# A gated mix of an S4D convolution and a GLU: a new table for the order of every engine

## The chip, the cores and the metric

The kernel runs on one core of a Trainium2 chip, in fp32 from end to end. A core has five engines with an instruction queue each, run in order: TensorE (PE in the profile, with its weight loads as PEld), VectorE (DVE), ScalarE (ACT), GpSimd (POOL) and SyncE (SP), which here only issues transfers to the DMA engines. An engine waits on semaphores for what other engines or transfers have to finish first. What counts is the device time of one execution in microseconds.

## The reference

One input u of 2048 positions by 448 channels goes through two branches and a gate. The first branch is a state-space convolution (S4D) of 256 states per channel, the second a GLU with 1792 hidden units.

```python
def _A_ref(u, log_A_real, A_imag, C_real, C_imag, log_dt, D_skip):
    dt = jnp.exp(log_dt)
    A = -jnp.exp(log_A_real) + 1j * A_imag
    C = (C_real + 1j * C_imag) * dt[:, None]
    P = jnp.exp((A * dt[:, None])[:, :, None] * pos[None, None, :])
    K = 2.0 * jnp.einsum("dn,dnl->dl", C, P).real
    L2 = 2 * L
    ...
    y = jnp.fft.irfft(Uf * Kf[None, :, :], L2)[:, :, :L]
    ...
    return y + u * D_skip[None, None, :]
...
    g = jnp.einsum("bsd,df->bsf", x, w_gate)
    u = jnp.einsum("bsd,df->bsf", x, w_up)
    h = _sigmoid(g) * u
    return jnp.einsum("bsf,fd->bsd", h, w_down)
...
g = _sigmoid((x * gate_w).sum(-1, keepdims=True))
return g * a + (1 - g) * b
```

## The kernel before

Three strands of work share the engines, and the program interleaves them.

**The GLU** has the largest part of TensorE. The positions are split in two halves H of 1024, the hidden units in 14 groups f of 128. fp32 accuracy is had from pairs of rounded numbers: each weight and input is split into a high and a low part (L1341 to L1348 for x, L1379 and L1381 for the weights), and three products of high and low parts replace one. `glu_mm` writes one 128x512 tile `gu` in PSUM with eleven matmuls (L1414 to L1419; two gu buffers); ACT takes a tanh of it into `sg` (L1398), DVE multiplies (L1400, L1403), and the result is split into `hh` and `hl` (L1405, L1406) or, in the groups named in `WHOLE`, kept whole in fp32. `glu_down` multiplies by w_down into the one PSUM tile `dn` (three matmuls a group, L1435 to L1437; one fp32 matmul, L1433, for a whole group), and DVE or ACT adds it, scaled by the gate, to `ob` (L1445, L1452).

**The convolution kernel** K is generated in 28 chunks `c` (`kgen`), 16 channels at a time, in two half chunks of 128 states (`half_chunk`). The phase of every state is a product of position and frequency on TensorE, one 128x512 tile `tp` in PSUM (T1, L1223). ACT rounds it to whole turns (L1227) into `cs` and writes the negated turns `nn` (L1229); TensorE adds these to the same tile (T2, L1232), so that a fraction of a turn is left; ACT reads that for cosine (L1234) and sine (L1235, and L1245 for both halves of the cosine). GpSimd makes the decay as powers (L1203 to L1216), DVE spreads them (`es`, L1252) and multiplies them with cosine and sine (L1266, L1269). Then 128 small matmuls (L1281, in the mode of 128x32 tiles) contract over the states into `kp`, and ACT copies that to `ke` (L1302). There are two `tp` buffers, one `nn`, one `es`, three `cs` and one `kp`.

**The transforms** replace the FFT by two stages of matrices, 64 by 32, over position: stage 1 (L812, matmuls on 64 rows of the array), a transpose (for the input through DMA, for the kernel on DVE, L826), a spectrum stage (L845, 64x64 tiles), the product with the spectrum of the input (L879, DVE), the inverse stage (L889, 64x64) and the way back (L926, 64 columns). The matrices of the outer stages come from DRAM in tables `ft` (for the input half `fu`) and `ftx`, 256 KB a load; the `fu` strand and `ftx` have one buffer each, so a load waits until the last matmul of the table before is done, and the first of the next waits for the load.

**What sets the order.** All operations are first recorded with their reads, writes and buffers. `Plan.order` gives each operation the rank that the table `PLACE` has for it: the key is the engine, the tile that is written and a priority, and the numbers are the ranks on that engine of the operations with this key, in order of recording. Each engine's queue is sorted by this rank (`queue`), and the queues are emitted as they stand. A rank is not a time: an engine that comes to an instruction too early waits on its semaphore. Buffers of a tag rotate in the order of recording. The table therefore sets, for each engine, what stands between a producer and its consumer, and nothing else in the program does.

## Time and profile before

| | us |
|---|---|
| median of three runs | 690.57 |
| lowest, highest | 689.83, 692.58 |
| span of the profiled execution | 688.4 |
| PE busy in it | 673.8 (98%) |
| DVE, ACT, POOL busy | 602.0 (87%), 510.0 (74%), 274.9 (40%) |

The profiled execution is one of its own, 2.2 us shorter than the median. Its granted TensorE clock is full throughout. A busy share says how much of the time an engine had an instruction in work; with overlapping instructions of one engine the busy times of the groups sum to more than that. What an engine waits for, and how long, stands in the views of waits and in brackets in the timeline.

### The profile page before, as it was taken

The page shows a single profiled execution, that of the slowest core. Times are in us where ns is not written, and L with a number is a line of the kernel's source. Part 1 is how long each engine was busy: PE and PEld are TensorE (multiplying, and loading weights), DVE is VectorE, ACT ScalarE, POOL GpSimd, SP SyncE. Part 2 cuts the span into 40 slices and gives each one's busy share as a digit, 9 for nine tenths or more (in the row PEclk, how much of TensorE's full clock was granted, in tenths as well). Part 3 has the DMA queues.
Part 4 walks back from the last instruction along what each step waited for, and adds up shares of the span by engine and source line. Part 5 has one row for each costly group of instructions (what it writes and reads, how often), then busy time and mean ns, then how long its engine had stood idle before and what let it go on. Part 6 is the DMA issues. An engine that isn't in the chain of part 4 may idle for free.

```text
span 688.4 us, 16283 instructions
## 1 busy us (share of the span) xinstructions
PE 673.8 (98%) x6588; PEld 483.1 (70%) x6588; DVE 602.0 (87%) x699; ACT 510.0 (74%) x928; POOL 274.9 (40%) x280
## 2 busy tenths in 40 slices
PE   9999999999999999999899999999999999999996
PEld 8776667877886687775556676788888766556873
DVE  5999999999999999989999789999973489577976
ACT  5677699899999999999999999999941352233110
POOL 0315268865447656675663845667000000000000
PEclk9999999999999999999999999999999999999999
DMA  9769342656896787737966974457948973979866
GB/s 252 180 177 246 87 108 70 153 138 237 186 182 157 177 215 178 225 112 177 193 171 144 233 199 90 140 168 184 180 100 202 271 235 124 312 246 241 166 179 165
DMA packets 97474, 123.84 MB, mean 180 GB/s; under 512 B 31096, under 2 KB 80568, under 8 KB 96376
## 3 DMA queue, kind: packets, MB, share of 16 engines
q1 hardware_dynamic: 97400, 122.81, 69.8%
q8 instruction: 52, 0.85, 0.5%
q14 instruction: 22, 0.18, 0.1%
HBM read 79.20 MB, written 43.58 MB: 178 GB/s over the span
## 4 chain that ended last, share of the span: by engine, by line
PE 73%; ACT 10%; DVE 8%; DMA 5%; issue 2%; SPq 1%; ACTq 0%; DVEq 0%
PE gu_gps L1414 9%; PE gu_gps L1415 8%; PE gu_gps L1416 8%; PE kp_egp L1281 6%; PE dn_gps L1433 5%; PE dn_gps L1435 4%; PE tp_egp L1232 4%; PE dn_gps L1436 4%; PE dn_gps L1437 4%; PE tp_egp L1223 4%; PE fps_fups L812 3%; PE gu_gps L1418 3%; PE gu_gps L1419 3%; PE fps_fups L845 2%; PE fps_fups L889 2%
## 5 line engine op out<-in xcount | busy, mean ns | idle before, releaser
L1414 PE MATMUL gu_gps<-xs_glu,wh_glu 128*128 128x512 f32 x336 | 144.5, 430 | 1.4 <-DVE hl_glu L1400 0.9
L1416 PE MATMUL gu_gps<-xs_glu,wl_glu 128*128 128x512 f32 x336 | 131.8, 392 | 0.0
L1415 PE MATMUL gu_gps<-xs_glu,wh_glu 128*128 128x512 f32 x336 | 131.7, 392 | 0.0
L1269 DVE TENSOR_TENSOR cs_eg<-cs_eg,es_eg 128x2048 f32<-128x2048 f32 x56 | 129.2, 2307 | 1.4
L1252 DVE TENSOR_TENSOR es_eg<-tb_eg 128x1024 f32<-128x1024 f32 x112 | 110.5, 1003 | 3.0 <-POOL tb_eg L1216 0.9
L1213 POOL TENSOR_TENSOR tb_eg<-tb_eg 128x96 f32<-128x96 f32 (+2 forms) x84 | 107.5, 1284 | 5.9
L1216 POOL TENSOR_TENSOR tb_eg<-tb_eg,bs_eg 128x32 f32<-128x32 f32 x84 | 83.9, 1001 | 5.8
L1414 PEld LDWEIGHTS gu_gps<-xs_glu,wh_glu 128*128 128x128 f32 x336 | 63.2, 188 | 30.2 <-issue 13.0
L1398 ACT ACTIVATE sg_glu<-gu_gps 128x512 f32<-128x512 f32 x56 | 33.7, 603 | 58.3 <-PE gu_gps L1419 58.3
L1266 DVE TENSOR_TENSOR cs_eg<-cs_eg,es_eg 128x1024 f32<-128x1024 f32 x56 | 70.5, 1260 | 7.2 <-ACT cs_eg L1245 6.0
L1229 ACT ACTIVATE nn_eg<-cs_eg 128x512 fp32r<-128x512 f32 x112 | 71.7, 640 | 4.5 <-PE tp_egp L1232 2.9
L1415 PEld LDWEIGHTS gu_gps<-xs_glu,wh_glu 128*128 128x128 f32 x336 | 63.3, 188 | 15.4 <-issue 4.8
L1416 PEld LDWEIGHTS gu_gps<-xs_glu,wl_glu 128*128 128x128 f32 x336 | 63.1, 188 | 14.5
L1452 DVE SCALAR_TENSOR_TENSOR ob_glu<-dn_gps,og,ob_glu 128x448 f32<-128x448 f32 x72 | 48.7, 676 | 25.1 <-PE dn_gps L1437 24.1
L1234 ACT ACTIVATE cs_eg<-tp_egp 128x512 f32<-128x512 f32 x112 | 66.5, 605 | 4.1 <-PE tp_egp L1232 3.6
L1227 ACT ACTIVATE cs_eg<-tp_egp 128x512 f32<-128x512 f32 x112 | 67.9, 607 | 1.6 <-PE kp_egp L1281 0.6
L1235 ACT ACTIVATE cs_eg<-tp_egp 128x512 f32<-128x512 f32 x112 | 67.3, 606 | 1.6 <-PE tp_egp L1232 1.4
L1245 ACT ACTIVATE cs_eg<-cs_eg,half_pi 128x1024 f32<-128x1024 f32 x56 | 65.2, 1165 | 0.4
L1281 PEld LDWEIGHTS kp_egp<-cs_eg 128*32 128x32 f32 x3584 | 51.5, 110 | 11.7 <-issue 6.3
L1281 PE MATMUL kp_egp<-cs_eg 128*32 128x64 f32 x3584 | 56.3, 220 | 0.5 <-issue 0.4
L1203 POOL MEMSET tb_eg<- 128x96 f32 x28 | 7.8, 285 | 116.4 <-DVE es_eg L1252 105.5
L1232 PE MATMUL tp_egp<-nn_eg,idn 128*128 128x512 f32 x112 | 49.7, 444 | 3.9 <-ACT nn_eg L1229 3.4
(161 smaller groups left out, 1326.2 us busy)
## 6 DMA issues: line engine op xcount, KB each, us to landing
shf<-fx_fu SPq DMA_DIRECT2D x16, 896.0 KB
fx_fu<-shf SPq DMA_DIRECT2D x16, 896.0 KB
us<-fx_fu SPq DMA_DIRECT2D x16, 896.0 KB
xr_glu<-in_w_dram SPq DMA_DIRECT2D x46, 256.0 KB
uax_fk<-us SPq DMA_DIRECT2D x16, 448.0 KB
ua_fk<-us SPq DMA_DIRECT2D x16, 448.0 KB
xr_glu<-in_w_dram SPq DMA_DIRECT2D x17, 224.0 KB
gt_pre<-in_u_dram SPq DMA_DIRECT2D x8, 448.0 KB
```

Source lines behind the costliest of these rows:

```text
L1213: pool(96 * m, lambda n=n, m=m: G.tensor_mul(g3(n + 1, m), g3(1, m), g3(n, 1).to_broadcast([128, 32, 3, m])))
L1216: pool(32, lambda e=e: G.tensor_mul(t(e + 1), t(e), b(3)))
L1227: op("Act", c_act(512, True), lambda: S.activation(cs[:, 1, ds, 32:96], block(tp), AF.Copy, bias=MAGIC), [tp], [(cs, ("s", i))], prio)
L1229: op("Act", c_act(512), lambda: S.activation(block(nn), cs[:, 1, ds, 32:96], AF.Copy, scale=-1.0, bias=MAGIC), [(cs, ("s", i))], [nn], prio)
L1232: op("PE", c_mm(532), lambda: T.matmul(tp.real, idn.real, nn.real, start=False, stop=True, skip_group_check=True), [nn, idn], [tp], prio)
L1252: V.tensor_mul(o.rearrange("p d (i k) -> p d i k", k=ny), x.unsqueeze(3).to_broadcast([128, 16, nx, ny]), y.unsqueeze(2).to_broadcast([128 ...
L1266: op("DVE", c_dve(1024), lambda: V.tensor_mul(cs[:, :, :, 0:32], cs[:, ::-1, :, 63:31:-1], es[:, :, 0:32].unsqueeze(1).to_broadcast([128, ...
L1269: op("DVE", c_dve(2048), lambda: V.tensor_mul(cs[:, :, :, 32:96], cs[:, :, :, 32:96], es[:, :, 32:96].unsqueeze(1).to_broadcast([128, 2, 1 ...
L1281: T.matmul(kp[32 * j:32 * j + 32, q], cs[:, z, 4 * j + q, 64:96], cs[:, z, 4 * j + q, 0:64], start=cs is parts[0] and z == 0 and q == 0, s ...
L1414: T.matmul(p.real, wh[:, k, cs], x[:, k], start=(k == 0), stop=False)
L1415: T.matmul(p.real, wh[:, k, cs], x[:, 4 + k], start=False, stop=False)
L1416: T.matmul(p.real, wl[:, k, cs], x[:, k], start=False, stop=False)
```

## The change

Only the numbers of `PLACE` differ. Operations, tiles, buffers, priorities and constants are the same, and so is the code below the table. The ranks of all five engines are new. Two of the keys, the contraction and the phase tiles on TensorE, in their first rows:

```diff
-    ('PE', 'kp', 20): (164, 198, 220, 245, 272, 296, 320, 341, 364, 390, 415, 438, 459, 479, 503, 520, 538, 558, 581,
...
-    ('PE', 'tp', 20): (105, 119, 112, 125, 134, 142, 137, 145, 153, 158, 155, 162, 165, 171, 167, 178, 177, 185, 186,
-        192, 194, 202, 199, 205, 207, 214, 209, 219, 218, 225, 223, 229, 232, 238, 236, 242, 243, 249, 247, 253, 256,
...
+    ('PE', 'kp', 20): (166, 200, 220, 245, 271, 298, 321, 342, 364, 391, 415, 438, 460, 480, 502, 522, 540, 559, 580,
...
+    ('PE', 'tp', 20): (106, 116, 108, 121, 134, 139, 136, 144, 152, 158, 155, 163, 165, 172, 168, 176, 179, 186, 180,
+        190, 193, 202, 194, 205, 207, 213, 211, 217, 218, 225, 222, 230, 232, 238, 234, 242, 244, 249, 247, 253, 256,
...
```

What the table does to the queues is told by the order of instructions. In the names, `tp_egp66` is the phase tile number 66, `kp_egp15` the contraction of chunk 15, `gu_gps` a GLU up tile, `dn_gps` a GLU down tile, and the number behind the underscore only tells tiles apart.

TensorE, around the contraction of chunk 15, which runs at 334 us in the trace of before. Before:

```order
L1281 MATMUL kp_egp15_4109<-cs_eg30_3924 32x64 x32
L1281 MATMUL kp_egp15_4109<-cs_eg31_4035 32x64 x32
L1223 MATMUL tp_egp66_4179<-pos_sb_72,phs_73 128x512
L1433 MATMUL dn_gps38_4097<-vh_glu13_3294,hl_glu19_3887 128x448
L1223 MATMUL tp_egp67_4191<-pos_sb_72,phs_73 128x512
L1232 MATMUL tp_egp66_4179<-nn_eg66_4189,idn_71 128x512
L1232 MATMUL tp_egp67_4191<-nn_eg67_4197,idn_71 128x512
L1414 MATMUL gu_gps58_4056<-xs_glu2_3221,wh_glu12_2626 128x512
```

After:

```order
L1223 MATMUL tp_egp66_4112<-pos_sb_72,phs_73 128x512
L1281 MATMUL kp_egp15_4117<-cs_eg30_3923 32x64 x32
L1281 MATMUL kp_egp15_4117<-cs_eg31_4037 32x64 x32
L1223 MATMUL tp_egp67_4186<-pos_sb_72,phs_73 128x512
L1414 MATMUL gu_gps58_4059<-xs_glu2_3293,wh_glu12_2738 128x512
L1415 MATMUL gu_gps58_4059<-xs_glu2_3293,wh_glu12_2738 128x512
L1416 MATMUL gu_gps58_4059<-xs_glu2_3293,wl_glu12_2785 128x512
L1418 MATMUL gu_gps58_4059<-xs_glu2_3293,wh_glu12_2738 128x512
L1419 MATMUL gu_gps58_4059<-xs_glu2_3293,wl_glu12_2785 128x512
L1232 MATMUL tp_egp66_4112<-nn_eg66_4195,idn_71 128x512
L1433 MATMUL dn_gps39_4203<-vh_glu11_3133,hl_glu18_3536 128x448
L1232 MATMUL tp_egp67_4186<-nn_eg67_4207,idn_71 128x512
```

T1 of tp66 now stands ahead of the contraction instead of behind it, and behind T1 of tp67 come five gu matmuls before the T2 of tp66, then one dn matmul before that of tp67. The dn matmul between the two T1s has moved away.

TensorE, some 24 instructions later, around the contraction of chunk 16 (346 us in the trace of before). Before:

```order
L1232 MATMUL tp_egp68_4221<-nn_eg68_4232,idn_71 128x512
L1433 MATMUL dn_gps39_4223<-vh_glu13_3294,hl_glu19_3887 128x448
L1414 MATMUL gu_gps59_4206<-xs_glu2_3221,wh_glu12_2626 128x512
L1415 MATMUL gu_gps59_4206<-xs_glu2_3221,wh_glu12_2626 128x512
L1416 MATMUL gu_gps59_4206<-xs_glu2_3221,wl_glu12_2729 128x512
L1232 MATMUL tp_egp69_4228<-nn_eg69_4240,idn_71 128x512
L1223 MATMUL tp_egp70_4252<-pos_sb_72,phs_73 128x512
L1281 MATMUL kp_egp16_4257<-cs_eg32_4080 32x64 x32
L1281 MATMUL kp_egp16_4257<-cs_eg33_4185 32x64 x32
```

After:

```order
L1232 MATMUL tp_egp68_4222<-nn_eg68_4249,idn_71 128x512
L1418 MATMUL gu_gps59_4225<-xs_glu2_3293,wh_glu12_2738 128x512
L1419 MATMUL gu_gps59_4225<-xs_glu2_3293,wl_glu12_2785 128x512
L1232 MATMUL tp_egp69_4238<-nn_eg69_4256,idn_71 128x512
L1223 MATMUL tp_egp70_4264<-pos_sb_72,phs_73 128x512
L1281 MATMUL kp_egp16_4268<-cs_eg32_4090 32x64 x32
L1281 MATMUL kp_egp16_4268<-cs_eg33_4188 32x64 x32
L1223 MATMUL tp_egp71_4338<-pos_sb_72,phs_73 128x512
```

The T1 of tp70 needs the tp buffer of tp68. Between the T2 of tp68 and it stood one dn matmul, three gu matmuls and the T2 of tp69; now it is two gu matmuls and the T2 of tp69.

TensorE, around the contraction of chunk 13 (near 306 us), where a stage-1 run of the transforms (L812, the mode of 64 rows) stands. Before:

```order
L1281 MATMUL kp_egp13_3768<-cs_eg26_3566 32x64 x32
L1281 MATMUL kp_egp13_3768<-cs_eg27_3686 32x64 x32
L812 MATMUL fps_fups51_3841<-fx_fu1_3158,ft_fu7_3704 128x224
L812 MATMUL fps_fups52_3842<-fx_fu1_3158,ft_fu7_3704 128x224
L812 MATMUL fps_fups51_3841<-fx_fu1_3158,ft_fu7_3704 128x224
L812 MATMUL fps_fups52_3842<-fx_fu1_3158,ft_fu7_3704 128x224
L1223 MATMUL tp_egp58_3854<-pos_sb_72,phs_73 128x512
L1433 MATMUL dn_gps35_3859<-vh_glu11_3212,hh_glu17_3113 128x448
L1223 MATMUL tp_egp59_3864<-pos_sb_72,phs_73 128x512
L1433 MATMUL dn_gps35_3859<-vh_glu12_3292,hl_glu17_3165 128x448
```

After:

```order
L1281 MATMUL kp_egp13_3772<-cs_eg26_3572 32x64 x32
L1281 MATMUL kp_egp13_3772<-cs_eg27_3691 32x64 x32
L1223 MATMUL tp_egp59_3850<-pos_sb_72,phs_73 128x512
L1414 MATMUL gu_gps56_3853<-xs_glu2_3293,wh_glu11_2427 128x512
L1415 MATMUL gu_gps56_3853<-xs_glu2_3293,wh_glu11_2427 128x512
L1416 MATMUL gu_gps56_3853<-xs_glu2_3293,wl_glu11_2501 128x512
L1433 MATMUL dn_gps35_3863<-vh_glu11_3133,hh_glu17_3121 128x448
L812 MATMUL fps_fups51_3870<-fx_fu1_3151,ft_fu7_3711 128x224
L812 MATMUL fps_fups52_3871<-fx_fu1_3151,ft_fu7_3711 128x224
L812 MATMUL fps_fups51_3870<-fx_fu1_3151,ft_fu7_3711 128x224
L812 MATMUL fps_fups52_3871<-fx_fu1_3151,ft_fu7_3711 128x224
L1414 MATMUL gu_gps57_3880<-xs_glu2_3293,wh_glu11_2427 128x512
```

The L812 run stood directly behind the contraction; now full-array matmuls (T1, gu, dn) stand between them, and the L812 run has full-array work on both sides.

## The prediction

> **What bounds the kernel now.** I read the page first: busy times, slices, chain.

> ```profile
> PE 673.8 (98%) x6588; PEld 483.1 (70%) x6588; DVE 602.0 (87%) x699; ACT 510.0 (74%) x928; POOL 274.9 (40%) x280
> PE   9999999999999999999899999999999999999996
> PE 73%; ACT 10%; DVE 8%; DMA 5%; issue 2%; SPq 1%; ACTq 0%; DVEq 0%
> ```

> TensorE is busy in 673.8 of 688.4 us, so a new order can take away 14.6 us at most: the waits, the start and the tail. It can also lengthen the 673.8. Next the stretches, to see where the idle time lies.

> ```profile
> core 0: us, PE busy (x) PEld busy (x) DVE busy (x) ACT busy (x) POOL busy (x), PEclk, DMA share, GB/s
> 300.00:360.00 60.00, 55.56 (x702) 34.61 (x701) 56.07 (x51) 57.51 (x105) 35.27 (x37) 1.00 0.77 179
> 360.00:500.00 140.00, 139.59 (x1806) 103.08 (x1806) 128.94 (x115) 135.75 (x248) 77.28 (x81) 1.00 0.68 165
> 500.00:640.00 140.00, 140.00 (x974) 93.87 (x973) 94.31 (x106) 47.08 (x92) 0.00 (x0) 1.00 0.76 217
> ```

> The columns behind each stretch are its length and the busy time of PE, weight loads, DVE, ACT, POOL. From 300 to 360 us TensorE idles 60.00 − 55.56 = 4.4 us; from 360 to 640 only 0.4. The clock is full, so it has no part here. In 300–360 ACT idles only 2.5 us: three engines are nearly full at once. Then TensorE's waits, the whole run first, then that stretch, then ACT's own there (in total, times, longest):

> ```profile
> PE tp_egp L1232 <- ACT nn_eg L1229: 3.4, 7, 0.9
> PE gu_gps L1414 <- DVE hl_glu L1400: 0.9, 1, 0.9
> PE fps_fups L926 <- DMA ftx_fk<-in_t1t_dram: 0.6, 1, 0.6
> PE gu_gps L1414 <- ACT sg_glu L1398: 0.4, 1, 0.4
> ...
> PE tp_egp L1232 <- ACT nn_eg L1229: 3.2, 6, 0.9
> PE tp_egp L1223 <- ACT cs_eg L1235: 0.9, 2, 0.6
> ...
> ACT nn_eg L1229 <- PE tp_egp L1232: 1.3, 5, 0.7
> ```

> The costliest wait is one round trip. T1 (L1223) writes a phase tile into PSUM; ACT rounds it (L1227) and negates (L1229); T2 (L1232) adds that back on TensorE. Then ACT reads the sum twice (L1234, L1235) and frees one of the two tp buffers. A T2 that comes too soon stops TensorE. Seen in the timeline (start, duration, what; in brackets the idle time before):

> ```profile
> 334.24 1.99 PE L1281 MATMUL kp_egp<-cs_eg 128*32 128x64 f32 x128
> 336.16 0.50 PE L1223 MATMUL tp_egp<-pos_sb,phs 97*128 97x512 f32 x1
> 336.49 0.92 PE L1433 MATMUL dn_gps<-vh_glu,hl_glu 128*128 128x448 f32 x2
> 336.90 0.74 PE L1223 MATMUL tp_egp<-pos_sb,phs 97*128 97x512 f32 x1
> 338.00 0.49 PE L1232 MATMUL tp_egp<-nn_eg,idn 128*128 128x512 f32 x1 [0.37 <-ACT nn_eg L1229]
> 339.28 0.50 PE L1232 MATMUL tp_egp<-nn_eg,idn 128*128 128x512 f32 x1 [0.78 <-ACT nn_eg L1229]
> 339.61 0.40 PE L1414 MATMUL gu_gps<-xs_glu,wh_glu 128*128 128x512 f32 x1
> 339.85 0.39 PE L1415 MATMUL gu_gps<-xs_glu,wh_glu 128*128 128x512 f32 x1
> ...
> 343.41 0.50 PE L1232 MATMUL tp_egp<-nn_eg,idn 128*128 128x512 f32 x1
> ...
> 345.19 0.39 PE L1232 MATMUL tp_egp<-nn_eg,idn 128*128 128x512 f32 x1
> 346.15 0.50 PE L1223 MATMUL tp_egp<-pos_sb,phs 97*128 97x512 f32 x1 [0.57 <-ACT cs_eg L1235]
> ```

> Both T2s, 1.28 us apart, wait for ACT, while independent gu matmuls (0.23 us from start to start) stand behind them. ACT needs for one round trip

> ```profile
> L1227 ACT ACTIVATE cs_eg<-tp_egp 128x512 f32<-128x512 f32 x112 | 67.9, 607 | 1.6 <-PE kp_egp L1281 0.6
> L1229 ACT ACTIVATE nn_eg<-cs_eg 128x512 fp32r<-128x512 f32 x112 | 71.7, 640 | 4.5 <-PE tp_egp L1232 2.9
> ```

> 0.61 + 0.64 = 1.25 us, if nothing else is queued on it.

> **The change part by part.** The table of places alone is new: the multiset of instructions on TensorE is the same, and nothing is added or removed. So there are five terms, made against the profiled 688.4 us; the median, 690.57, lies 2.2 above, and I carry the difference over.

> *1. The round trips, 300–360 us.* At the place above (in the order printed ahead) T1 of tp66 now goes before the contraction, and five gu matmuls of 0.23 us stand between T1 of tp67 and T2 of tp66. From T1 to T2 of tp66 TensorE now has 1.99 + 0.23 + 5 × 0.23 = 3.4 us of work, against 1.5 before (336.16 to 338.00, less 0.37); that is more than 1.25 plus one queued ACT instruction of 0.6. Counting in this way for each of the twenty phase tiles tp54 to tp73, the mean work between T1 and T2 rises from 2.93 to 3.27 us, and over the whole program the pairs with under 2.0 us fall from seven to two. The waits up to 345 us (3.2 + 0.9, less the 0.6 at 346.15: 3.5 us) should nearly all go. Against that stands the place at tp70: its T1 needs the buffer of tp68. From the start of T2 of tp68 to where that T1 can start was 2.2 us of work (343.41 to 345.19, and 0.39), and it still waited 0.57; now it is four matmuls of 0.23, 0.9 us. ACT needs T2's 0.5 and two instructions of 0.6, 1.7 us, at best, and took 2.2 + 0.6 = 2.8 here: a wait of 0.8 to 1.9. I take 1.1, so 0.5 more than before, and 0.5 for new small ones. Net −2.5. Bounds: 0, if ACT, idle 2.5 us in all and partly for T2 itself, cannot run closer; −4.4, if all idle time goes.

> *2. More changes of tile shape on TensorE.* Counted over the whole order, the runs of one shape (full array, 64 rows, 64 columns, 64x64, 128x32) rise from 176 to 184: six more interruptions of full-array work. What one costs:

> ```profile
> 179.71 0.39 PE L1419 MATMUL gu_gps<-xs_glu,wl_glu 128*128 128x512 f32 x1
> 180.03 2.27 PE L1281 MATMUL kp_egp<-cs_eg 128*32 128x64 f32 x128
> 182.23 0.50 PE L1414 MATMUL gu_gps<-xs_glu,wh_glu 128*128 128x512 f32 x1
> 182.57 0.39 PE L1415 MATMUL gu_gps<-xs_glu,wh_glu 128*128 128x512 f32 x1
> ...
> 565.75 0.98 PE L845 MATMUL fps_fups<-fx_fu,m_sb 64*64 64x448 f32 x8
> 566.66 0.50 PE L1414 MATMUL gu_gps<-xs_glu,wh_glu 128*128 128x512 f32 x1
> ...
> 589.43 0.93 PE L845 MATMUL fps_fups<-fx_fu,m_sb 64*64 64x448 f32 x8
> 590.18 1.03 PE L845 MATMUL fps_fkps<-fx_fk,m_sb 64*64 64x448 f32 x8
> ```

> Entering, 179.71 to 180.03 is 0.32 instead of 0.23; leaving, 182.23 to 182.57 is 0.34: together 0.20. A run of eight L845 takes 0.91 alone (565.75 to 566.66) and 0.75 next to its like (589.43 to 590.18), so up to 0.16 more: 0.20 to 0.36. Six of them cost 1.2 to 2.2; I take 1.6. All of it is on the path, since TensorE sets the end. [...]

> *3. Table loads of the transforms.* The stage tables ft and ftx have one buffer, 256 KB a load, so TensorE needs other work between the last reader of one and the first of the next. Two loads that were waited for, in the chain:

> ```profile
> 162.55 3.19 DMA ft_fu<-in_s1t_dram
> 672.81 3.97 DMA ftx_fk<-in_t1t_dram
> ```

> By the order, with the starts of the rows above as its prices, one ft load had under 3.5 us of cover before (3.14; it waited 0.19); now there are four ft loads (3.14, 3.14, 3.20, 3.43) and two of ftx (3.48 each; before 8.30 and 3.71). At 3.19 plus 0.14 until the matmul starts, the ft loads cost 0.2 + 0.2 + 0.1, 0.3 more than before; the ftx loads at 3.97 cost 0.5 each, and 0 at 3.48: 0.2 each. Together +0.7, between 0.2 and 1.6. [...]

> *4. Single waits that lose their cause.* The 0.9 for hl and the 0.4 for sg stand here:

> ```profile
> 68.32 0.50 PE L1414 MATMUL gu_gps<-xs_glu,wh_glu 128*128 128x512 f32 x1 [0.87 <-DVE hl_glu L1400]
> ...
> 657.39 0.50 PE L1414 MATMUL gu_gps<-xs_glu,wh_glu 128*128 128x512 f32 x1 [0.42 <-ACT sg_glu L1398]
> ```

> By the order, the work between producer and consumer grows there by 2 and 3.9 us, so −0.8 and −0.4. The last 25 TensorE instructions and the tail keep their order:

> ```profile
> 683.68 0.69 DVE L1452 SCALAR_TENSOR_TENSOR ob_glu<-dn_gps,og,ob_glu 128x448 f32<-128x448 f32 x1 [0.96 <-PE dn_gps L1437]
> ```

> so these 4.7 us behind 683.68 stay.

> *5. The first 60 us.* SP now issues four small loads (D_skip) ahead of weights, and DVE some fills; a sigmoid stands behind a weight split. No wait is sure: between 0 and +1, I take +0.3.

> Sum: −2.5 + 1.6 + 0.7 − 1.2 + 0.3 = −1.1. Span 687.3; predicted time 690.57 − 1.1 = **689.5 us**. The 3.9 us that DVE idles in 300–360 I count as nothing: no TensorE wait there names DVE.

> **The rivals.**

> *The tight place takes the gain back.* ACT has 57.5 us of work in these 60; a wait taken from one T2 comes back at tp70 and after. For it: 0.9 us of cover where 2.2 did not do, and ACT's place in its queue must fit. Against it: ACT also idles on T2 (1.3 us), which earlier T1s cure. Term 1 becomes 0: 690.57 + 1.4 = 692.0, no change.

> *The table loads come late: slower.* Each of the six short loads queues on SP behind stores and shares 77% busy queues. At 4.3 us a load, the six wait 1.2, 1.2, 1.1, 0.9, 0.8 and 0.8: 6.0, less 0.2 before. With the other terms at −1.8: 690.57 − 1.8 + 5.8 = 694.6. It decides from about 4.2 us a load; for it speaks 3.97 at 672 us, against it 3.19 at 162 us.

> *Nearly all waits go: faster.* All 4.4 us of the stretch and the other waits of 0.9, 0.4, 0.6 and 0.2 vanish, no new one comes, and the shape changes cost 1.2: 690.57 − 6.5 + 1.2 = 685.3. For it: ACT and DVE have no more work than TensorE there. Against: at tp70 the order itself shows the next wait.

> *The table does not decide.* If waits were set by something else than the order of the engines (by transfers, say), the time stays: 690.6.

> **How the numbers follow.** Forecast 0.45, tight place 0.2, slow loads 0.13, all waits gone 0.17, table without effect 0.05. One part in two hundred, 3.5 us, is about what a measurement of this kernel can tell from no change. Faster than that: the third rival and the lower tail of the forecast, 0.2; slower: the second rival, 0.13, say 0.14; between, 0.66. The range reaches from near the fast rival, 686.0, to short of the slow one, 693.8. All bounds of terms 1 to 5 at once give 686.4 to 694.2; the forecast's own range, half of that to each side, is 687.5 to 692.

> **What would show it.** Right: in 300–345 us TensorE waits for L1229 under 1 us instead of 2.5 or more, one wait of about a microsecond at the T1 of tp70, TensorE busy 675.0 to 676.0 instead of 673.8, waits for ft and ftx of 0.5 to 2 us, and the tail unchanged. Term 1 is wrong if the stretch still idles 4 us; term 2 if busy time stays at 673.8 or lies above 677; term 3 if ft waits are absent or above 3. A new wait of several microseconds in the first 60 us would break the forecast.

## The result: slower by 2.3%

The changed kernel takes 707.36 us (706.6 to 708.2) against 690.68 us (689.8 to 692.6) before: ratio 1.0232, 95% interval 1.0212 to 1.0252. The forecast was 689.5 us, with a range from 686.0 to 693.8. In the profiled executions the span grew from 688.4 to 706.4 us, by 18.0 us.

The profile page of the changed kernel, with the lines that answer to those shown of before:

```profile
PE 678.9 (96%) x6588; PEld 489.2 (69%) x6588; DVE 598.7 (85%) x699; ACT 509.8 (72%) x928; POOL 254.7 (36%) x280
...
PE   9999999999999999999698998988999999999996
...
PEclk9999999999999999999889999999999999999999
...
q8 instruction: 52, 0.85, 0.5%
```

TensorE is busy 5.1 us longer and idle 12.9 us longer, and for the first time its granted clock (PEclk) dips, in the middle of the run. The stretches and TensorE's waits say where:

```profile
300.00:360.00 60.00, 52.45 (x673) 33.49 (x673) 52.35 (x49) 51.15 (x93) 37.75 (x45) 0.91 0.81 183
360.00:500.00 140.00, 129.42 (x1633) 93.18 (x1633) 114.48 (x99) 125.15 (x230) 55.83 (x72) 0.98 0.59 145
500.00:640.00 140.00, 140.00 (x1073) 97.18 (x1075) 97.51 (x111) 59.33 (x111) 0.00 (x0) 1.00 0.70 203
```

```profile
PE kp_egp L1281 <- issue: 11.9, 4, 4.8
PE gu_gps L1416 <- issue: 3.5, 1, 3.5
PE tp_egp L1232 <- ACT nn_eg L1229: 2.1, 6, 0.8
PE tp_egp L1223 <- ACT cs_eg L1234: 1.3, 4, 0.5
PE fps_fups L812 <- DMA ft_fu<-in_s1t_dram: 1.2, 1, 1.2
```

From 360 to 500 us, where TensorE idled 0.4 us before, it now idles 10.6. The waits that the forecast spoke of did shrink (L1229 from 3.4 to 2.1). What is new stands above them: 15.4 us in five waits on "issue", that is, the profile shows no engine and no transfer of the program that ended them. The largest in the timeline:

```profile
344.17 1.98 PE L1281 MATMUL kp_egp<-cs_eg 128*32 128x64 f32 x125
350.95 0.42 PE L1281 MATMUL kp_egp<-cs_eg 128*32 128x64 f32 x3 [4.80 <-issue]
351.30 0.80 PE L1223 MATMUL tp_egp<-pos_sb,phs 97*128 97x512 f32 x1
351.90 0.63 PE L1414 MATMUL gu_gps<-xs_glu,wh_glu 128*128 128x512 f32 x1
...
388.30 0.39 PE L1416 MATMUL gu_gps<-xs_glu,wl_glu 128*128 128x512 f32 x1 [3.46 <-issue]
```

TensorE stops after 125 of the 128 matmuls of one contraction, and the last three read no other tiles than those before them, so their operands were there; after the stop a gu matmul takes 0.63 instead of 0.40 us.

```
instruction   fetch began   fetch ended   TensorE went on   after its end
  7105          348.43        349.44          350.95             1.51
  7873          385.94        386.90          388.30             1.39
  8897          427.59        428.96          430.52             1.56
  9665          459.79        461.01          462.47             1.46
 10433          492.39        493.68          495.13             1.45
```

Each stop ends 1.4 to 1.6 us after its fetch has landed. No fetch of the two kernels begins more than 284 instructions, little more than a line, ahead of the line's first.

**Why it comes late.** I count from when a fetch could be asked for. No trace shows that moment; my estimate is 284 instructions ahead, the earliest that any was seen to begin, and the fetch before it landed. From there to its first byte the 52 fetches of the changed kernel take between 0 and 9.1 us, and this goes with the megabytes that other transfers move in that time: correlation 0.93, and 0.90 in the kernel before. No fetch that waited over 4 us in the changed kernel had less than 0.9 MB moving meanwhile. A longer wait sees more bytes move in any case, so the correlation alone does not show the cause; the experiments have to.

How long TensorE can wait for a fetch depends on the contractions. One is 128 matmuls and 128 weight loads, a whole line, in 2.0 us (1.99 at 334 us in the kernel before). In the changed kernel, from when a fetch could be asked for to when its line was needed, 18 us and more passed where no contraction or hardly any of one lay between, some 12 to 18 us where a part of one did, and 4 to 10 us where nearly all of one did (over 210 of its 256 instructions). The five stops are of the last kind: 4.8 to 7.4 us of time, and fetches that began after 4.5 to 8.4 us.

**The kernel before lived on the edge.** There, too, five lines were begun 1.35 to 1.51 us after their fetch ended, with no time to spare (at 240, 350, 390, 450 and 479 us). Only one was waited for, which its list of waits showed:

```profile
PE kp_egp L1281 <- issue: 0.4, 1, 0.4
```

### The profile page after: what moved, and what is told of

It is laid out like the page before. It is cut to its first block, busy times and chain, and to the rows that moved or that the text cites. A ratio compares the mean times of both kernels' runs of the same rounds, so it can differ in the third digit from the quotient of the medians.

```text
span 706.4 us, 16268 instructions
## 1 busy us (share of the span) xinstructions
PE 678.9 (96%) x6588; PEld 489.2 (69%) x6588; DVE 598.7 (85%) x699; ACT 509.8 (72%) x928; POOL 254.7 (36%) x280
## 4 chain that ended last, share of the span: by engine, by line
PE 84%; ACT 8%; issue 3%; DVE 2%; DMA 2%; SPq 0%; ACTq 0%; DVEq 0%
PE gu_gps L1414 10%; PE gu_gps L1415 10%; PE gu_gps L1416 10%; PE dn_gps L1433 8%; PE kp_egp L1281 7%; PE tp_egp L1223 4%; PE dn_gps L1435 4%; PE tp_egp L1232 4%; PE dn_gps L1436 4%; PE dn_gps L1437 4%; PE gu_gps L1418 3%; PE fps_fups L812 3%; PE gu_gps L1419 3%; PE fps_fups L845 2%; PE fps_fups L889 2%
## 5 line engine op out<-in xcount | busy, mean ns | idle before, releaser
L1414 PE MATMUL gu_gps<-xs_glu,wh_glu 128*128 128x512 f32 x336 | 148.1, 441 | 0.1
L1415 PE MATMUL gu_gps<-xs_glu,wh_glu 128*128 128x512 f32 x336 | 133.1, 396 | 0.0
L1213 POOL TENSOR_TENSOR tb_eg<-tb_eg 128x192 f32<-128x192 f32 (+2 forms) x84 | 105.9, 1262 | 6.2
L1414 PEld LDWEIGHTS gu_gps<-xs_glu,wh_glu 128*128 128x128 f32 x336 | 63.9, 190 | 33.8 <-issue 19.7
L1229 ACT ACTIVATE nn_eg<-cs_eg 128x512 fp32r<-128x512 f32 x112 | 72.8, 650 | 7.0 <-PE tp_egp L1232 6.2
L1398 ACT ACTIVATE sg_glu<-gu_gps 128x512 f32<-128x512 f32 x56 | 33.7, 602 | 59.1 <-PE gu_gps L1419 59.0
L1415 PEld LDWEIGHTS gu_gps<-xs_glu,wh_glu 128*128 128x128 f32 x336 | 64.0, 190 | 16.0 <-issue 6.0
L1227 ACT ACTIVATE cs_eg<-tp_egp 128x512 f32<-128x512 f32 x112 | 68.0, 615 | 8.9 <-PE tp_egp L1223 5.0
L1416 PEld LDWEIGHTS gu_gps<-xs_glu,wl_glu 128*128 128x128 f32 x336 | 63.7, 190 | 14.6
L1281 PE MATMUL kp_egp<-cs_eg 128*32 128x64 f32 x3584 | 57.4, 220 | 12.1 <-issue 11.9
L1234 ACT ACTIVATE cs_eg<-tp_egp 128x512 f32<-128x512 f32 x112 | 67.5, 613 | 1.9 <-PE tp_egp L1232 1.4
L1235 ACT ACTIVATE cs_eg<-tp_egp 128x512 f32<-128x512 f32 x112 | 67.7, 613 | 0.2 <-PE tp_egp L1232 0.2
L1281 PEld LDWEIGHTS kp_egp<-cs_eg 128*32 128x32 f32 x3584 | 51.9, 110 | 22.6 <-issue 21.6
L1216 POOL TENSOR_TENSOR tb_eg<-tb_eg,bs_eg 128x32 f32<-128x32 f32 x84 | 63.5, 758 | 5.9
L1452 DVE SCALAR_TENSOR_TENSOR ob_glu<-dn_gps,og,ob_glu 128x448 f32<-128x448 f32 x72 | 48.8, 678 | 16.3 <-PE dn_gps L1437 14.1
L1232 PE MATMUL tp_egp<-nn_eg,idn 128*128 128x512 f32 x112 | 51.5, 460 | 2.2 <-ACT nn_eg L1229 2.1
```

The source lines that it names most:

```text
L1213: pool(96 * m, lambda n=n, m=m: G.tensor_mul(g3(n + 1, m), g3(1, m), g3(n, 1).to_broadcast([128, 32, 3, m])))
L1227: op("Act", c_act(512, True), lambda: S.activation(cs[:, 1, ds, 32:96], block(tp), AF.Copy, bias=MAGIC), [tp], [(cs, ("s", i))], prio)
L1229: op("Act", c_act(512), lambda: S.activation(block(nn), cs[:, 1, ds, 32:96], AF.Copy, scale=-1.0, bias=MAGIC), [(cs, ("s", i))], [nn], prio)
L1232: op("PE", c_mm(532), lambda: T.matmul(tp.real, idn.real, nn.real, start=False, stop=True, skip_group_check=True), [nn, idn], [tp], prio)
L1235: op("Act", c_act(512, True), lambda: S.activation(cs[:, 1, ds, 32:96], block(tp), AF.Sin, scale=TWO_PI), [tp], [(cs, ("s", i))], prio, ta ...
L1281: T.matmul(kp[32 * j:32 * j + 32, q], cs[:, z, 4 * j + q, 64:96], cs[:, z, 4 * j + q, 0:64], start=cs is parts[0] and z == 0 and q == 0, s ...
```

## The experiments

Two theories. F: TensorE runs out of instructions, since fetches queue behind bulk transfers and contractions use up a line at once. O: the loss lies in the new order itself, in its round trips, buffers and waits. Line numbers in the runs whose edit adds a line are higher by one. Times without an interval are of a single execution. The waits on issue in the runs below stand, counted in TensorE's queue as above, at the start of a line in 21 cases out of 22; the one that does not, 1.2 us at 157 us, is in the run with SP's old order.

### The lines shifted, the order untouched (kernel before)

```diff
-WAKE = 24
+WAKE, EXTRA = 24, 32
...
                 T.matmul(wake[:, :128], ones.real, ones.real, start=True, stop=True)
+            for k in range(EXTRA): T.matmul(wake[32 * (k % 4):32 * (k % 4) + 32, :64], ones[:, 0:32], ones[:, 0:64], start=True, stop=True)
```

> The kernel before, every engine in its old order, with 32 small fp32 matmuls (128x32 tiles, 128 instructions of TensorE with their weight loads) added behind the wake-up matmuls at the start; their results are not read. Theory F (TensorE runs out of instructions: lines of 256 instructions are fetched by transfers of 16 KB, a fetch waits behind the bulk transfers, and a contraction uses up a whole line in 2 us): the added 128 instructions shift all later lines by half a line, so other fetches meet the contractions; five or more waits on 'issue' of 1 to 8 us each, 15 to 35 us in all, 705 to 727 us. Theory O (the loss of the changed kernel lies in its order of work: round trips, buffers, waits between engines): the order is the old one, so only the added matmuls cost, 1 to 3 us: 691 to 694 us.

719.86 us against 692.2: slower by 28 us, without any change of order. TensorE's waits:

```profile
PE gu_gps L1415 <- issue: 5.5, 1, 5.5
PE kp_egp L1282 <- issue: 5.3, 2, 4.3
PE gu_gps L1416 <- issue: 4.1, 1, 4.1
PE tp_egp L1233 <- ACT nn_eg L1230: 3.4, 7, 0.9
PE gu_gps L1417 <- issue: 2.3, 1, 2.3
```

The wait for L1229 (here L1230) is as before, 3.4 us, and 17.2 us of waits on issue have come (with two smaller ones 19.2). One more wait, of 1.3 us at 344 us, is put down to an ACT instruction, but it stands at the start of a line as well, 1.6 us behind the end of its fetch. The added matmuls themselves delay the first gu matmul by 0.2 us (9.49 instead of 9.29). O falls by this run.

### The same shift on the changed kernel

The edit is the same, on the changed kernel.

> The changed kernel in its own order, with the same 32 small matmuls (128 instructions) added behind the wake-up matmuls. In the first such run, on the kernel before, they delayed the first GLU matmul by 0.2 us only. Theory F: the waits on 'issue' leave the five places of the changed kernel (351, 388, 431, 462, 495 us), since other lines meet the contractions there, and come at others; at least three of the five shrink to under 0.5 us, and new ones of over 1 us stand before 300 us; in all 10 to 35 us of waits, 700 to 730 us. Theory O (the waits belong to those places of the order): the five stay, 707 to 709 us.

718.96 us. The stops at 351, 388, 431, 462 and 495 are gone or moved:

```profile
201.89 0.37 PE L1282 MATMUL kp_egp<-cs_eg 128*32 128x64 f32 x2 [6.17 <-issue]
...
236.60 0.80 PE L1416 MATMUL gu_gps<-xs_glu,wh_glu 128*128 128x512 f32 x1 [3.94 <-issue]
```

The others over 1 us are 3.1 at 273, 2.7 at 456 and 3.7 at 520; the waits on issue come to 19.9 us in all, as F said. A wait of 1.4 us at 342, put down to an ACT instruction, stands at the start of a line too. The shifted kernel before had its largest at 203 (5.5), 238 (4.1), 273 (2.3) and 522 us (4.3): two different orders with the same shift stop at nearly the same four places, and each order stops elsewhere without it. Where the lines fall decides, more than the order.

### An extra transfer (kernel before)

```diff
+    ('SP', 'dum', 99): (186.3, 186.6),
...
+    dum = [dt_([96, 1024], f"dum{i}") for i in halves]
+    for i in halves: dma(lambda i=i: dum[i].real, lambda: pos[0:96, 0:1024].bitcast(F32), 96 * 4096, [pos], [Res(name="dum", real=dum[i].real)], 99)
```

> The kernel before, in its old order, with two extra transfers of 393 KB each (a constant table from SBUF to a DRAM buffer that nobody reads) issued at about 339 us, behind the load of fx_fu that stands there; nothing waits for them. Theory F: the instruction fetch that landed just in time at 348.3 us queues behind 0.79 MB more, at some 0.2 MB per us 3.5 to 4.5 us later, and TensorE stops on 'issue' for 2.5 to 4.5 us near the end of the contraction at 346.6 us; if it stops for over 3 us, matmuls behind it run at a lower clock; 693 to 698 us. Theory O: no engine waits for these transfers and the DMA queues are not the bound, so 690 to 692 us and no new wait there.

694.43 us in one execution, as F said, where the kernel before lay between 689.8 and 695.9 in this series; so the time proves little, and the trace has to tell. SP issued the two transfers at 337.6 and 338.2 us. The fetch in question waited some 5.5 us instead of 3.9 and landed at 347.99; TensorE went on 1.35 us later:

```profile
347.73 0.40 PE L1417 MATMUL gu_gps<-xs_glu,wl_glu 128*128 128x512 f32 x1
349.34 0.39 PE L1233 MATMUL tp_egp<-nn_eg,idn 128*128 128x512 f32 x1 [1.21 <-ACT cs_eg L1228]
```

(the row names an ACT instruction as releaser; 1.35 us behind the fetch's end is where the stops on issue end). So 0.79 MB more delayed the fetch by 1.6 us, not by 4, and the stop was 1.2 us, not 2.5 to 4.5; the fetch began when some 0.2 MB of the transfers asked for had not yet started, so it does not strictly queue behind all of them. A second stop, of 2.63 us at 481, came where the kernel before had a fetch without time to spare. Whether that one comes from the extra transfers was not settled. At the first place the trace of this one execution shows a fetch, and TensorE with it, delayed behind transfers that nobody waits for; the exact rule of the fetch's waiting is not shown.

### The transfers' order alone put back (changed kernel)

```diff
-    ('SP', 'acc', 5): (165, 171, 174, 192, 191, 193, 199, 197,),
+    ('SP', 'acc', 5): (194, 189, 172, 197, 193, 191, 215, 199,),
```

and so for all rows of SP.

> The changed order on TensorE, ACT, DVE and GpSimd, and the old order of the transfers on SP. Theory F: TensorE's instructions stand as in the changed kernel, so the lines meet the contractions at the same places, but the transfers ahead of each fetch are others: the five waits on 'issue' of 4.8, 3.5, 1.8, 2.1 and 3.2 us do not all stay; at least two of them change by over 1 us, 690 to 708 us. Theory O: the order on the computing engines is the changed one, so the loss stays: 705 to 709 us.

717.4 us, outside what either theory expected. The stops on issue did change as F says: the one of 4.8 us is now 2.3 (at 358), and those at 388, 431, 462 and 495 are under 0.2. (The other wait on issue, 1.2 us at 157, is not at the start of a line and has another cause, not known.) But data now come late for the engines:

```profile
PE tp_egp L1232 <- ACT nn_eg L1229: 7.2, 7, 5.1
PE fps_fups L845 <- ACT fx_fu L762: 5.6, 1, 5.6
PE dn_gps L1435 <- DVE ob_glu L1452: 4.9, 3, 3.3
```

SP's order belongs to the other engines' order, so the time of this run decides nothing.

### The changed order up to 344 us, then the old one

For every engine, the operations that the changed kernel has issued up to a chunk's contraction keep their changed order, and the rest follow in the old order. The row of the contractions with the cut at chunk 16, against before:

```diff
-    ('PE', 'kp', 20): (164, 198, 220, 245, 272, 296, 320, 341, 364, 390, 415, 438, 459, 479, 503, 520, 538, 558, 581,
+    ('PE', 'kp', 20): (166, 200, 220, 245, 271, 298, 321, 342, 364, 391, 415, 438, 460, 480, 502, 522, 538, 558, 581,
```

> All five engines in the changed order up to the contraction of chunk 16 (some 344 us), and from there in the old order. In the two traces the changed kernel leads by 2.4 us at that contraction and loses its 20 us behind it. Theory F: the fetches behind the cut meet the old order again, so no wait on 'issue' over 1 us and the lead is kept: 688.3 us, 687 to 690. If the lead itself moves TensorE against the transfers, one of the five fetches that were just in time before (at 238.6, 348.3, 388.8, 448.7 and 477.2 us) may now come 1 to 3 us late: up to 692. Theory O: the same 688.3, since each stretch keeps its own waits.

692.91 us, ratio 1.0007 (0.9987 to 1.0028). One stop is left, 4.80 us at 351, as in the changed kernel; the four behind it are gone (the largest is 0.34). So the stop at 351 is made ahead of 344 us. With the 4.2 us at half clock behind it, it outweighs the lead: in the trace this kernel is 2.3 us ahead at the contraction of chunk 16 and 2.9 us behind at the next, though the medians do not differ. F expected the lead to be kept; it failed for the one fetch that straddles the cut.

### The same with the cut one chunk earlier

The cut is at the contraction of chunk 15, 332 us.

> The changed order up to the contraction of chunk 15 (332 us), one chunk earlier than in the run with the cut at 344 us, and the old order behind. That run lost 4.8 us at one fetch, whose backlog was issued between 332 and 344 us. Theory F: with the old order of transfers from 332 us on, that fetch comes in time, no wait on 'issue' over 1 us is left, and the lead of 2.2 us at that contraction is kept: 2 us faster than before, ratio 0.996 to 0.998. If the lead alone puts it out of step again: a wait of 1 to 5 us at 350 us and no gain. Theory O: as the run with the cut at 344, no gain, ratio 1.000 to 1.002.

687.95 us, ratio 0.9943 (0.9920 to 0.9967): faster than both kernels, and by about 4 us instead of the 2 that F gave. The trace shows less (a lead of 2.8 us at chunk 16 and 2.1 at chunk 17, and spans that differ by 1.2); the rest is not explained. What SP issues around the fetch, first with the cut at 344, then at 332:

```profile
336.98 0.76 SPq L712 DMA_DIRECT2D phs<-phd  x1
337.79 1.47 SPq L712 DMA_DIRECT2D ft_fu<-in_s1t_dram  x1
339.35 2.11 SPq L712 DMA_DIRECT2D acc<-ob_glu  x3
342.51 0.33 SPq L712 DMA_DIRECT2D xr_glu<-in_w_dram  x1
```

```profile
334.81 1.67 SPq L712 DMA_DIRECT2D bs_eg<-bsd  x1
346.22 1.50 SPq L712 DMA_DIRECT2D phs<-phd  x2
```

With the early cut nothing is issued from 336.5 to 346.2 us. The fetch could then begin at 339.6 and begins at 344.5 us; with the late cut it could begin at 340.1 and begins at 348.6. Its stop falls from 4.80 to 0.99 us:

```profile
347.40 0.50 PE L1415 MATMUL gu_gps<-xs_glu,wh_glu 128*128 128x512 f32 x1 [0.99 <-issue]
```

### Contractions of half as many instructions

```diff
-                for z in range(2):
+                for z in range(1):
...
-                            T.matmul(kp[32 * j:32 * j + 32, q], cs[:, z, 4 * j + q, 64:96], cs[:, z, 4 * j + q, 0:64],
+                            T.matmul(kp[32 * j:32 * j + 32, q], cs[:, 0, 4 * j + q, 64:96], cs[:, 0:2, 4 * j + q, 0:64],
```

The sine half as weights is left out, so both kernels with this edit compute another K. On the changed kernel:

> The changed kernel, with the contraction of each chunk in half as many matmuls, each twice as wide: the sine half of the states is left out as weights, and every matmul streams cosine and sine side by side (128 columns instead of 64), so that a contraction is 128 instructions instead of 256 and about as long (1.9 us). K is wrong by that; all other work, order and transfers are the same. Theory F: no contraction uses up a line of 256 instructions in 2 us any more, so all waits on 'issue' go (under 0.5 us in all, before 15.4), the clock stays full, and the time falls from 707 to 687 to 691 us, less or more by what the contractions themselves change. Theory O: the order, and with it the loss, is unchanged: 703 to 709 us.

On the kernel before:

> The kernel before with the same half-as-many, twice-as-wide contractions (the sine half left out as weights). It is the one to compare the changed kernel with the same contractions with. Theory F: 689 to 691 us plus or minus what the contractions change, and the changed kernel stands against it as the prediction said when it knew of no fetch: 1.1 us faster, at least not over 2 us slower. Theory O: the changed kernel stays 13 us or more slower than this one.

685.50 us for the changed kernel (0.9898 of before, 0.9875 to 0.9921) and 689.92 for the kernel before (0.9968, 0.9952 to 0.9984). TensorE's waits, changed order first:

```profile
PE tp_egp L1232 <- ACT nn_eg L1229: 2.3, 6, 1.1
PE fps_fups L812 <- DMA ft_fu<-in_s1t_dram: 1.7, 1, 1.7
PE tp_egp L1223 <- ACT cs_eg L1234: 1.3, 4, 0.5
```

```profile
PE tp_egp L1232 <- ACT nn_eg L1229: 3.8, 8, 0.9
PE fps_fups L812 <- DMA ft_fu<-in_s1t_dram: 1.7, 4, 0.5
...
PE tp_egp L1223 <- ACT cs_eg L1235: 0.9, 2, 0.6
```

No wait on issue is left in either, though a contraction takes as long (64 matmuls in 1.96 us), and no line is begun less than 2 us after its fetch has landed. Without these stops the changed order is 4.4 us faster than the old one, instead of 16.7 slower.

## Why the prediction was wrong

**The account of the 18.0 us.** Waits on issue: 15.4 against 0.4, so +15.0. The clock: the trace's clock records grant half speed for 10.2 us from 348.4, 3.4 from 389.4 and 3.4 from 495.2; of these 17.1 us, 2.5 fall into the stop itself, and the other 14.5 lose about half (a gu matmul 0.43 us from start to start instead of 0.23), some +7.2. The rest is 18.0 − 22.2 = −4.2. The two kernels with half contractions differ by −4.4 in their medians and by −5.3 in their profiled spans (689.2 and 683.9), so the account closes to about 1 us. The windows around the largest stop (granted clock third from the end):

```profile
345.00:351.00 6.00, 1.20 (x83) 1.04 (x72) 5.93 (x6) 1.81 (x3) 2.61 (x2) 0.79 1.02 292
351.00:359.00 8.00, 7.22 (x25) 3.50 (x28) 3.43 (x5) 4.85 (x10) 7.21 (x16) 0.52 0.38 128
```

In this kernel stops of 3.15, 3.46 and 4.80 us came with half speed, those of 1.83 and 2.12 did not. Between these no length decides: in the other runs stops of 2.31, 2.33 and 2.63 us were followed by half speed, and one of 2.73 was not. The stretches at half speed last 10.24, 3.41 and 3.41 us, the first three times the others; it begins 2.3 us into its stop, the others 1.1 and 0.1 us behind the end of theirs. What starts a stretch, and what sets its length, is not shown.

**The step that failed** is at the start of the part-by-part working: nothing is added or removed, "so there are five terms". A sixth was missing: TensorE's own instructions come by transfers (52 of 16 KB here), and a new order moves both when a line is used up and what is on the DMA queues then. It was put at nothing, and cost 15.0 us of stops and some 7 us of clock. The evidence was on the page of the kernel before (`q8 instruction: 52, 0.85, 0.5%`, and one wait on issue at a contraction), and I quoted the contraction's rows without counting its 256 instructions. That the clock is full and has no part was true of the kernel before alone. The rival for slower had the right kind of cause, a transfer that comes late, and the wrong transfer: the table loads cost 0.6 us. The last rival, waits set by transfers, named that cause in brackets, but took it that the time would then stay.

**The 2.2 us between span and median, carried over,** did not hold exactly: here they are 706.4 and 707.36, so the medians differ by 16.7 us where the spans differ by 18.0. An execution's span is some 1.8 us shorter than its time, and the profiled execution of the changed kernel, 708.21 us, was the longest of its four.

**Term 1, the round trips, −2.5.** Right in mechanism, too large over the whole stretch. From 300 to 345 us TensorE waits 1.0 us for L1229 instead of 3.2, and the lead of the changed kernel grows from 0.2 us at the contraction of chunk 13 to 2.5 at chunk 14 and stands at 2.4 at chunk 16. The tight place at tp70 is there, but smaller: its T1 waited 0.48, not 1.1. Part of its price comes behind chunk 16, where the T2 of tp71 waits next (0.78; 1.07 with half contractions). In the two kernels with half contractions, TensorE idles from chunk 13 to chunk 18 3.4 us in the changed order and 4.6 in the old one, so 1.2 us of waits are saved net.

**Term 2, changes of shape, +1.6.** Wrong in size, and not what decides the busy time. The changes rose from 176 to 184 as counted, and over all of them what TensorE spends above an ordinary step rose by 0.6 to 0.9 us, by what one takes for an ordinary step, in the two kernels with half contractions. But its busy time fell there, from 672.8 to 669.8. A part of that may be the first matmul behind a wait, which runs 0.1 to 0.25 us longer (at 68.32 us in the kernel before the next follows after 0.34 us instead of 0.23): there are 19 instead of 25 waits of over 0.1 us. At least 1.5 us are not explained.

**Term 3, table loads, +0.7.** Right in sum, by luck: waits for ft and ftx are 1.23 and 0.12 us against 0.19 and 0.57, so +0.6, but all of it in one ft load, where +0.3 was forecast, while ftx fell instead of rising. With half contractions the ft waits are 1.7 us in both orders, and the term is nothing.

**Term 4, single waits, −1.2.** Right: the 0.9 for hl and the 0.4 for sg are gone in the changed kernel.

**Term 5, the first 60 us, +0.3.** Wrong in sign: with the matmuls done by 60 us priced at their ordinary steps, the changed kernel is 1.3 us ahead there (2.1 with half contractions). At the first contraction it leads by 2.15 us (112.78 against 114.92), 0.9 of it from term 4; small waits at 34, 55 and 95 us are gone too. From there to chunk 13 the lead falls to 0.2 us, 1.2 of that by the one ft load; the rest is not worked out.

So the five terms say −1.1, and the order, freed of these stops, gives −4.4; the stops and the clock behind them add some 21 to 22 us. One figure of the prediction's working is off by half a microsecond and changes nothing: half the way from 689.5 to 686.4 is 688.0, not 687.5.

## What to carry to other kernels

When a profile shows an engine waiting on "issue", count its instructions: if the stops lie a multiple of 256 apart in its queue, as here, look whether an instruction transfer has ended just before each of them, here 1.4 to 1.6 us; if so, it runs out of instructions, and no dependency in the program explains that. Here a contraction used up a line of 256 instructions in 2.0 us, and a fetch took up to 9.1 us to begin; so a burst of many short matmuls should be weighed together with the transfers issued in the 10 us ahead of it. A tuned order can rest on fetches that land just in time; shifting the lines by some dummy instructions at the start, at 0.2 us, shows in one run how much can hang on such luck (28 us here).

## What was not expected of the hardware

An instruction fetch of 16 KB, itself 0.9 to 1.7 us long, took up to 9.1 us to begin in the changed kernel and 11.7 in the one before, counted from my estimate of when it could be asked for, with 1.8 and 2.1 MB of other transfers moving meanwhile. TensorE needed another 1.4 to 1.6 us from its end to the next matmul in the five stops. With two transfers of 0.79 MB in all that no engine waits for, TensorE stopped for 1.2 us more through a fetch. And three stops of over 3 us were paid once more in the clock: 14.5 us at half speed behind them.
